# Filling matmuls of 512 and 256 columns in place of 128 in an attention and mixture-of-experts kernel

## The chip, the core and the metric

The kernel runs on one core of a Trainium2 chip. The metric is the device time of one execution in microseconds (us); several executions are timed and their median is given. One further execution is recorded by the hardware profiler, with its own time and its span, the stretch from the first to the last instruction of the program.

TensorE multiplies matrices (PE in the profile, PEld for its weight loads), VectorE is DVE, ScalarE is ACT, GpSimd is POOL, and SyncE (SP) issues nearly all data transfers.

## The reference

For each of 8 batches and 8 heads, a softmax over 32 memory slots pools keys and values, and the queries attend to the pooled ones:

```python
a = softmax(phi)                                  # (8, 8, 576, 32)
k_m = einsum('bhsm,bhsd->bhmd', a, k)             # pooled keys, 32 x 64
v_m = einsum('bhsm,bhsd->bhmd', a, v)
attn = softmax(q @ k_m.T / sqrt(64))
x = (attn @ v_m), laid out as (4608, 512)
```

The 4608 rows then go through a soft mixture of 8 experts with 4 slots each:

```python
logits = x @ phi_moe                              # (4608, 32)
slot_input = softmax_over_rows(logits).T @ x      # (32, 512)
slot_out[e] = relu(slot_input[e] @ w1[e]) @ w2[e] # 512 -> 1024 -> 512
out = softmax_over_slots(logits) @ slot_out       # (4608, 512)
```

All of it is float32.

## The kernel before

The work is put down as a list of operations, each with its engine, an assumed cost in us, the tiles it reads and writes, and a due time. A planner (`Plan.order`, L70, with `BatchPlan.order`, L256) simulates the engines and fixes the order in which each engine's instructions are issued; the order is static when the kernel runs. Each engine works through its own list in that order and waits where an input is late.

Per batch there are: the loads of phi, k, v and q (`load`, L481, all issued by SyncE; the DMA line in the profile is L483); the maximum of phi on VectorE (L536), its spreading by transposes and products on TensorE (L544, L558), the subtraction on GpSimd (L574), the exponential on ScalarE (L580), row sums on GpSimd (L587) and TensorE (L597); the pooling of keys and values as 144 small matmul records (L624); scaling on ScalarE (L640, L647), transposes (L658) and the routing product (L667); the scores (L735, two groups of 32 records), the softmax over VectorE, GpSimd and ScalarE (L749 to L799), transposes (L810), logits (L830), and the contribution to the slots (L913 to L963). Work of neighbouring batches overlaps. After the last batch the slot inputs are merged (SIM, L1096), the experts run (first layer L1163, second layer L1210) on weights that arrive 1 MB at a time in the arena space that the batches have left, and the output products (L1346) are copied and stored. L1317 is a product with 128x128 weights ahead of the output.

Where TensorE has no real work, the planner puts in filling products (`fill`, L497): products of a constant tile of ones by itself, into a PSUM bank that nothing reads. They have the priority `FILL`, behind all else, and every one is ready from the start. Two rules in `Plan.order` decide about them:

```python
look = self.LOOK if pri < FILL else self.FILL_LOOK      # 0.05 or 0.5
_, t, i = min(x for x in near if ops[x[2]][0] == e and x[1] <= t + look)
```

When a fill would be next, any real TensorE operation that is due within `FILL_LOOK` = 0.5 us is taken in its place; else one fill is issued and TensorE counts as taken for the fill's cost, `WC` = 0.3 us. Fills left over after the last real TensorE operation are dropped. `NWARM` = 250 are offered.

Of the kernel before, what the change touches and what calls it, by code (L numbers as in the profile page):

```python
# [16 lines left out]
PE, DVE, ACT, POOL, SP = range(5)  # L17
FILL = 10 ** 6


class Plan:
# [19 lines left out]
    def add(self, eng, cost, fn, r=(), w=(), also=(), pri=None, dma=0.0, slack=0.0):  # L41
        i = len(self.ops)
        deps = set()
        tiles = set()
        for x in r:
            for key in x:
                tiles.add(key[0])
                if key in self.last_w:
                    deps.add(self.last_w[key])
        for x in w:  # L50
            for key in x:
                tiles.add(key[0])
                if key in self.last_w:
                    deps.add(self.last_w[key])
                deps.update(self.reads.get(key, ()))
        for x in w:
            for key in x:
                self.last_w[key] = i
                self.reads[key] = []
        for x in r:  # L60
            for key in x:
                self.reads.setdefault(key, []).append(i)
        deps.discard(i)
        tiles = [t for t in tiles if t.pool is not None]
        for t in tiles:
            t.users += 1
        need = tiles + [t for t in also if t not in tiles]
        self.ops.append((eng, cost, fn, deps, i + self.bias if pri is None else pri, dma, tiles, need, slack))
# [212 lines left out]
def kernel(  # L281
# [30 lines left out]
    P = 128  # L312
# [28 lines left out]
    banks = [psum.tile([P, 512], F32, name=f"bank{i}") for i in range(4)]  # L341
# [56 lines left out]
    def entry(si):  # L398
# [36 lines left out]
    ident, maskhp, maskc, rep, repa, ones, mphd = (  # L435
        x.ap for x in (ident_b, maskhp_b, maskc_b, rep_b, repa_b, ones_b, mphd_b)
    )
    NWARM = 250
    WC = 0.3
    C_EXP = 0.8  # L440
    S_SLACK = 0.6

# [49 lines left out]

    warm = Tile(ap=banks[3][:, :P])

    def fill(n, pri, r=()):  # L497
        for _ in range(n):
            add(
                PE, WC,  # L500
                lambda: nc.tensor.matmul(  # L501
                    warm.ap, ones, ones,
                    start=True, stop=True,
                ),
                r=[ones_b, *r], w=[warm], pri=pri,
            )

    fill(NWARM, FILL)

    load(lambda: mphi_b.ap, moe_phi.rearrange("(c x) n -> x c n", x=P), 65536, mphi_b, pri=first("mphi"))  # L510

# [904 lines left out]
```

## Time and profile before

| What | us |
|---|---|
| median of 3 runs | 219.62 |
| lowest and highest | 218.26 to 220.39 |
| profiled execution, its own time | 218.71 |
| its span | 216.9 |
| TensorE busy (matmul) | 181.1 |
| VectorE busy | 135.9 |
| GpSimd busy | 88.9 |
| ScalarE busy | 83.0 |

The page shows busy times, then the span in 40 slices with a digit for the busy tenths of each; PEclk is the granted clock of TensorE in tenths. A row of a group or of the timeline has the engine, the source line, the operation, output and inputs by name, their shapes (for a matmul first the weights), and the count; the timeline puts start and length in us ahead, and in brackets behind how long the engine had stood idle and what ended that. "issue" stands where nothing that the profile records was waited for. A row of the windows has the stretch, its length, then for each engine the busy time with the number of instructions in brackets, then the granted clock, the DMA's share and its GB/s. A float32 product leaves two matmul records and two weight loads.

### The profile page before, as it was taken

How to read it: one execution, taken by the hardware profiler on the slowest of the kernel's cores; microseconds unless marked ns; L12 is line 12 of the kernel's file. 1: busy time of each engine (PE TensorE's matmuls, PEld its weight loads, DVE VectorE, ACT ScalarE, POOL GpSimd, SP SyncE). 2: the span in 40 equal slices, each digit the busy share in tenths (PEclk: the TensorE clock that was granted, in tenths of full speed). 3: DMA queues.
4: the chain of work that ended last, by engine and by line, in shares of the span. 5: the costliest groups of instructions: out<-in, count | busy, mean ns of one | idle time of the engine just before them, and what ended most of it. 6: DMA issues, size and time to landing. Idle time of an engine off the chain costs nothing.

```text
span 216.9 us, 6965 instructions
## 1 busy us (share of the span) xinstructions
PE 181.1 (83%) x3044; PEld 121.0 (56%) x3044; DVE 135.9 (63%) x246; ACT 83.0 (38%) x224; POOL 88.9 (41%) x96
## 2 busy tenths in 40 slices
PE   7697879979699989997999999989999967876700
PEld 6586559555366565654765657666555644643300
DVE  3335495988579798895759786549704850266700
ACT  2023306165066283672382946510102411146500
POOL 3381839487568575869265499000000000000000
PEclk9799997999979999997699999999999999999975
DMA  6999999999999999999943988699999999059997
GB/s 215 382 381 388 380 389 378 392 379 384 380 380 363 390 389 387 352 393 410 390 196 104 415 288 364 199 412 410 408 409 409 410 407 397 38 201 410 412 418 301
DMA packets 28174, 76.53 MB, mean 353 GB/s; under 512 B 1776, under 2 KB 5872, under 8 KB 28144
## 3 DMA queue, kind: packets, MB, share of 16 engines
q1 hardware_dynamic: 28144, 76.09, 92.6%
q8 instruction: 24, 0.39, 0.8%
q14 instruction: 6, 0.05, 0.1%
HBM read 66.65 MB, written 9.44 MB: 351 GB/s over the span
## 4 chain that ended last, share of the span: by engine, by line
PE 41%; DMA 19%; DVE 10%; ACT 8%; POOL 7%; SPq 6%; issue 4%; DVEq 0%; ACTq 0%; POOLq 0%
DMA arena<-in_moe_w_dram 11%; DMA arena<-in_phi_dram 8%; PE bank L1163 7%; PE kvbank L624 6%; PE scbank L735 6%; SPq L483 6%; PE bank L501 4%; DVE arena L1360 3%; PE scbank L1346 2%; PE bank L913 2%; PE kvbank L1210 2%; ACT arena L580 2%; PE bank L830 2%; POOL arena L794 2%; ACT arena L1358 2%
## 5 line engine op out<-in xcount | busy, mean ns | idle before, releaser
L501 PE MATMUL bank<-ones 128*128 128x128 f32 x232 | 38.6, 317 | 1.1 <-DVE ones L446 1.1
L501 PEld LDWEIGHTS bank<-ones 128*128 128x128 f32 x232 | 34.5, 227 | 4.2 <-issue 3.0
L587 POOL TENSOR_TENSOR arena<-arena 128x128 f32<-128x128 f32 (+2 forms) x32 | 23.4, 731 | 12.3 <-ACT arena L580 10.4
L703 DVE STREAM_TRANSPOSE arena<-top 128x1152 f32<-128x1152 f32 x16 | 21.7, 1360 | 10.6 <-DMA top<-in_q_dram 10.6
L574 POOL TENSOR_TENSOR arena<-arena 128x1152 f32<-128x1152 f32 x8 | 21.1, 2632 | 15.0 <-ACT arena L569 14.9
L771 POOL TENSOR_TENSOR arena<-arena,smx 128x576 f32<-128x576 f32 x16 | 18.5, 1159 | 14.3 <-DVE smx L766 14.3
L624 PE MATMUL kvbank<-arena 64*32 64x128 f32 x1152 | 21.9, 279 | 2.3 <-issue 1.2
L735 PE MATMUL scbank<-arena 32*32 32x288 f32 x512 | 21.2, 424 | 2.3 <-issue 2.1
L624 PEld LDWEIGHTS kvbank<-arena 64*32 64x32 f32 x1152 | 16.6, 107 | 7.4 <-issue 3.8
L749 DVE STREAM_TRANSPOSE arena<-scbank 128x576 f32<-128x576 f32 x16 | 12.3, 769 | 11.5 <-PE scbank L735 11.5
L815 ACT COPY arena<-bank 96x384 f32<-96x384 f32 x32 | 14.7, 483 | 12.3 <-PE bank L810 12.3
L536 DVE TENSOR_REDUCE arena<-arena 128x128 f32<-128x1152 f32 x8 | 17.4, 2179 | 2.6 <-DMA arena<-in_phi_dram 2.6
L794 POOL TENSOR_TENSOR arena<-arena,ssm 128x576 f32<-128x576 f32 x16 | 18.2, 1155 | 1.5 <-DVE ssm L790 1.3
L1210 PE MATMUL kvbank<-arena 128*32 128x256 f32 x256 | 16.1, 383 | 3.3 <-DMA arena<-in_moe_w_dram 3.2
L810 PE MATMUL bank<-ident,arena 128*96 128x128 f32 x96 | 16.0, 290 | 0.7 <-DVE arena L887 0.4
L799 DVE STREAM_TRANSPOSE arena<-arena 128x576 f32<-128x576 f32 x16 | 12.1, 758 | 5.1 <-POOL arena L794 5.1
L1163 PE MATMUL bank<-arena,SIM 128*32 128x256 f32 x256 | 14.2, 380 | 0.7 <-DVE SIM L1096 0.7
L735 PEld LDWEIGHTS scbank<-arena 32*32 32x32 f32 x512 | 8.1, 107 | 8.6 <-issue 3.1
L810 PEld LDWEIGHTS bank<-ident,arena 128*96 128x96 f32 x96 | 10.0, 132 | 5.0 <-issue 1.1
L1210 PEld LDWEIGHTS kvbank<-arena 128*32 128x32 f32 x256 | 7.3, 109 | 9.6 <-DMA arena<-in_moe_w_dram 5.3
L766 DVE TENSOR_REDUCE smx<-arena 128x18 f32<-128x576 f32 x16 | 11.8, 736 | 0.2
L776 ACT ACTIVATE arena<-arena 128x576 f32<-128x576 f32 x16 | 11.0, 690 | 2.1 <-POOL arena L771 2.1
(117 smaller groups left out, 266.1 us busy)
## 6 DMA issues: line engine op xcount, KB each, us to landing
arena<-in_moe_w_dram SPq DMA_DIRECT2D x32, 1024.0 KB, 11.2
arena<-in_k_dram SPq DMA_DIRECT2D x8, 1152.0 KB, 10.1
arena<-in_v_dram SPq DMA_DIRECT2D x8, 1152.0 KB, 12.6
top<-in_q_dram SPq DMA_DIRECT2D x8, 1152.0 KB, 11.0
out_dram<-arena SPq DMA_DIRECT2D x11, 768.0 KB, 6.5
arena<-in_phi_dram SPq DMA_DIRECT2D x8, 576.0 KB, 11.8
out_dram<-arena SPq DMA_DIRECT2D x3, 256.0 KB, 2.3
arena<-in_moe_phi_dram SPq DMA_DIRECT2D x1, 64.0 KB, 9.0
```

The costliest lines, as they stand in the source:

```text
L501: lambda: nc.tensor.matmul(warm.ap, ones, ones, start=True, stop=True,),
L536: lambda: nc.vector.tensor_reduce(mx.ap, ph().rearrange("p c j m -> p c m j"), axis=AX.X, op=ALU.max),
L574: lambda: nc.gpsimd.tensor_tensor(ph(), ph(), mb.ap.unsqueeze(2).to_broadcast([P, C, J, M]), op=ALU.subtract),
L587: plus = lambda o, x, y: nc.gpsimd.tensor_tensor(o, x, y, op=ALU.add)
L624: nc.tensor.matmul(acc.ap[M * c: M * c + M, a, : 2 * D], ph()[h0: h0 + HALF, c, j, :], kv()[h0: h0 + HALF, :, c, j * D: j * D + D], start= ...
L703: nc.vector.transpose(qT.ap.rearrange("p (i u y) -> p u i y", i=2, y=Y), qt.ap[:, h * QT_SZ: h * QT_SZ + QT_SZ].rearrange("p (u i x) -> p ...
L735: nc.tensor.matmul(scb.ap[M * c: M * c + M, r, :JY], kT.ap[h0: h0 + Y, i * P + M * c: i * P + M * c + M], qT[c // 2].ap.rearrange("p (i c ...
L771: lambda: nc.gpsimd.tensor_tensor(exv(), exv(), bc(mx), op=ALU.subtract),
L794: lambda: nc.gpsimd.tensor_tensor(exv(), exv(), bc(sm), op=ALU.mult),
L810: nc.tensor.transpose(tp.ap[:T, t * P: t * P + P], aT.ap[:, x: x + T], ident)
L1163: nc.tensor.matmul(hb.ap[NS * j: NS * j + NS, :256], SIM.ap[:, 2 * i + c, NS * e: NS * e + NS], wv[:, c, 256 * j: 256 * j + 256], start=(e ...
L1210: nc.tensor.matmul(pacc.ap[NS * x: NS * x + NS, h, :HD], hT()[:, 4 * t + i0 + j, NS * e: NS * e + NS], wv()[:, j, t, col: col + HD], start ...
```

## The change

`fill` takes a width. The first 14 fills multiply the ones by four copies of the ones side by side (512 columns, read by a broadcast), and the other 130 by two copies (256 columns). The assumed cost becomes 0.04 + 0.0021 times the columns: 1.115 us and 0.578 us. The tile that the fills write is the whole PSUM bank where it was its first 128 columns. Nothing else in the list of operations is changed; since the fills' costs enter the planner's simulation, the order of other work may come out otherwise.

```diff
-    NWARM = 250
-    WC = 0.3
+
+    NWIDE, NWARM = 14, 130
...
-    warm = Tile(ap=banks[3][:, :P])
-
-    def fill(n, pri, r=()):
+    warm = Tile(ap=banks[3])
+
+    def fill(n, w, pri, r=()):
         for _ in range(n):
             add(
-                PE, WC,
+                PE, 0.04 + 0.0021 * w,
                 lambda: nc.tensor.matmul(
-                    warm.ap, ones, ones,
+                    warm.ap[:, :w].rearrange("p (x y) -> p x y", y=P), ones,
+                    ones.unsqueeze(1).to_broadcast([P, w // P, P]),
                     start=True, stop=True,
                 ),
                 r=[ones_b, *r], w=[warm], pri=pri,
             )
 
-    fill(NWARM, FILL)
+    fill(NWIDE, 512, FILL)
+    fill(NWARM, 256, FILL)
```

## The prediction

> **What bounds the kernel now.** I read the page first, then the chain of work that ended last, then TensorE's timeline and the windows with their instruction counts.
>
> ```profile
> PE 181.1 (83%) x3044; PEld 121.0 (56%) x3044; DVE 135.9 (63%) x246; ACT 83.0 (38%) x224; POOL 88.9 (41%) x96
> PEclk9799997999979999997699999999999999999975
> q8 instruction: 24, 0.39, 0.8%
> PE 41%; DMA 19%; DVE 10%; ACT 8%; POOL 7%; SPq 6%; issue 4%; DVEq 0%; ACTq 0%; POOLq 0%
> L501 PE MATMUL bank<-ones 128*128 128x128 f32 x232 | 38.6, 317 | 1.1 <-DVE ones L446 1.1
> ```
>
> TensorE is the busiest engine and holds 41% of the chain. Its filling products (L501) are 232 of 3044 matmul records: a float32 product leaves two, each with a weight load, so 116 products ran, of the 250 allowed. The q8 row matters below: 24 packets carry 0.39 MB, about 16 KB each, while TensorE has 3044 + 3044 = 6088 instructions. That is 254 instructions, or 127 matmul records with their loads, to a packet.
>
> The chain shows the stages:
>
> ```profile
> 11.43 16.62 DMA arena<-in_phi_dram
> 28.07 2.12 DVE arena L536
> 56.33 1.72 issue
> 167.44 18.93 DMA arena<-in_moe_w_dram
> ```
>
> Until 28.07 us the inputs of the third batch set the pace: what TensorE does before that is covered by the DMA. Up to about 145 us the chain runs through the batches' work, much of it on TensorE. Late there means late release of the arena, hence late loading of the expert weights (last piece 167.44 + 18.93), and those loads end just before the outputs. So I carry lateness of TensorE between 31 and 107 us to the end one for one.
>
> The third row is the odd one: "issue", 1.72 us in which nothing seen was waited for. TensorE's timeline has seven such holes (brackets hold the idle time before the row):
>
> ```profile
> 26.38 1.73 PE L624 MATMUL kvbank<-arena 64*32 64x128 f32 x102 [0.76 <-issue]
> 45.48 0.16 PE L597 MATMUL bank<-maskhp,arena 128*128 128x2 f32 x1 [0.96 <-issue]
> 51.85 0.43 PE L624 MATMUL kvbank<-arena 64*32 64x128 f32 x10 [0.32 <-issue]
> 58.05 0.40 PE L735 MATMUL scbank<-arena 32*32 32x288 f32 x1 [1.72 <-issue]
> 72.53 1.19 PE L735 MATMUL scbank<-arena 32*32 32x288 f32 x29 [0.41 <-issue]
> 86.04 0.67 PE L624 MATMUL kvbank<-arena 64*32 64x128 f32 x30 [0.17 <-issue]
> 99.14 0.19 PE L935 MATMUL bank<-repa,arena 96*128 96x32 f32 x1 [1.16 <-issue]
> ```
>
> They cut runs of equal matmuls in two, so no data can be the reason. Counting TensorE's matmuls from the start up to the first, third, fourth and last hole (the count is in brackets), and taking one microsecond inside the fourth:
>
> ```profile
> 0.00:25.65 25.65, 20.91 (x349) 0.93 0.97 348
> 0.00:39.50 39.50, 32.45 (x603) 0.91 1.00 360
> 0.00:51.54 51.54, 43.07 (x857) 0.93 1.02 366
> 0.00:56.34 56.34, 47.55 (x985) 0.94 1.02 368
> 0.00:97.99 97.99, 85.70 (x1745) 0.95 1.03 373
> 57.00:58.00 1.00, 0.00 (x0) 0.00 (x0) 0.00 (x0) 0.00 (x0) 0.00 (x0) 1.00 1.06 359
> ```
>
> 349, 857, 985 and 1745 lie at multiples of 127 from one another (4 x 127 = 508; 128; 11 x 127 = 1397 against 1396). The holes are the edges of instruction packets: TensorE has used one up and the next has not come. From one edge to the next release passes 58.05 - 51.85 = 6.20 us and 51.85 - 45.48 = 6.37 us; the unheld edge at 603 was passed at 39.5 and the next opened at 45.48, 5.98 us later. So the rule I use is: an edge opens about 6.0 us after the last was passed, 6.2 if that one held, while the DMA is full (share 1.06 in the last row). A packet worked off faster ends in a hole. In the last row all five engines stand still: such a hole is not hidden.
>
> [...]
>
> **The change part by part.** First the number of fills. The planner takes a fill only when no real TensorE work is due within 0.5 us, and costs it at 0.3 us before, 0.04 + 0.0021 x 512 = 1.115 and 0.578 us after. Its gaps keep their length, so fewer, longer fills go in. The fills by stage:
>
> ```profile
> 0.00:7.00 7.00, 3.90 (x18) 3.71 (x18) 1.00 0.72 255
> 7.00:24.00 17.00, 9.34 (x58) 8.44 (x58) 0.90 1.07 385
> 24.00:39.20 15.20, 6.71 (x38) 6.24 (x38) 0.89 1.06 381
> 39.20:105.50 66.30, 5.57 (x32) 5.08 (x33) 0.93 1.04 383
> 105.50:146.00 40.50, 8.33 (x54) 6.85 (x53) 0.98 0.77 289
> ```
>
> To 7 us: 9 fills, 2.7 us of plan, become 3 wide ones. To 24 us: 29 fills, 8.7 us, lie in seven gaps, five of them of one or two fills which still take one whole wide fill, so 11 and not 8. That uses up all fourteen. To 39.2 us: 19 fills, 5.7 us, become 10 of 256 columns; to 105.5 us 16 become about 10. In records, 76 - 28 = 48 are gone by 24 us, 114 - 48 = 66 by 39 us, about 78 by 105.5 us.
>
> Second, the time that fills hold TensorE. Warm, the row of 128 columns at 189.06 (below) has 8 records in 1.05 us, about 0.13 each, 0.25 us a product, 0.83 of its planned 0.3. The nearest row for 256 columns with 128x128 weights is L1317 at 188.12: 4 records before the next start at 189.06, 0.235 each, 0.47 us a product, 0.81 of the planned 0.578. A straight line gives 0.9 us for 512 columns, 0.81 of the plan. Time per planned gap is thus the same: nought, bounds -1 us (two per cent of 38.6 busy, rounded up) and +1 us (a fill of 512 overshoots its gap by up to 0.6 us, and the gaps before 28 us lie under the DMA; only the short gaps after it count, with 0.08 us each).
>
> Third, the edges. With 48 to 68 records gone, each edge falls on later work. The first then lies near 349 + 50, inside the x102 run of L624; a hole like the longest seen is covered by VectorE's piece that starts at 28.07 and takes 2.12, on which TensorE waits anyway. For the next ones I take counts from before at the places where they land:
>
> ```profile
> 0.00:37.80 37.80, 30.75 (x543) 0.91 1.00 359
> 0.00:40.40 40.40, 33.35 (x666) 0.92 1.00 361
> 0.00:50.40 50.40, 41.94 (x799) 0.93 1.02 366
> 0.00:54.50 54.50, 45.72 (x922) 0.94 1.02 367
> ```
>
> The edge at 476 lands on 476 + 66 = 542, passed at 37.8; the next opens at 43.8. The edge at 603 lands on 669, reached at 40.4 after a dense run of L624 and L735: a hole of 3.4 us. The edge at 730 lands on 798. Before needs 10.0 us from 40.4 to there, 0.96 of it a hole, so 9.04: reached at 52.8, open since 43.8 + 6.2 = 50.0, no hole. The edge at 857 lands on 925; 4.1 - 0.32 = 3.8 us later, at 56.6, while it opens at 52.8 + 6.0 = 58.8: a hole of 2.2 us. Together 5.6 us against 0.96 + 0.32 + 1.72 = 3.0 before: +2.6 us. The later holes I take as they are (0.41 + 0.17 + 1.16), since a batch is a little over two packets and the edges drift through it in either kernel. Bounds: -4.7 (all holes after 39 us gone) and +4.
>
> Fourth, the clock. It fell to half after two of the holes, and these pairs show the same work at half and at full clock:
>
> ```profile
> 60.84 1.50 PE L830 MATMUL bank<-arena 128*32 128x192 f32 x12
> 74.02 0.85 PE L830 MATMUL bank<-arena 128*32 128x192 f32 x12
> 100.10 2.17 PE L735 MATMUL scbank<-arena 32*32 32x288 f32 x32
> 96.33 1.20 PE L735 MATMUL scbank<-arena 32*32 32x288 f32 x32
> 102.20 1.53 PE L624 MATMUL kvbank<-arena 64*32 64x128 f32 x48
> 94.20 0.94 PE L624 MATMUL kvbank<-arena 64*32 64x128 f32 x48
> 104.76 1.92 PE L501 MATMUL bank<-ones 128*128 128x128 f32 x8
> 189.06 1.05 PE L501 MATMUL bank<-ones 128*128 128x128 f32 x8
> 188.12 1.10 PE L1317 MATMUL bank<-arena,rep 128*128 128x256 f32 x4 [0.64 <-DVE arena L1312]
> ```
>
> The losses are 0.65 + 0.97 + 0.59 + 0.87 = 3.1 us, over one dip near 60 us and one twice as long from 100 us: about 1.0 us for each of three stretches. With two large holes instead I expect two stretches, 2.1 us: -1.0 us. Bounds: -3.1 (no dip left) and +2 (two stretches more).
>
> The sum: 0 + 2.6 - 1.0 = +1.6 us. The profiled execution took 218.71 us with a span of 216.9; with the term it is 220.3. It was below the median of the runs, 219.62; against that the forecast is **221.2 us**, 0.7% slower.
>
> **The rivals.** *The edges land well and the clock holds.* Fewer instructions pass through the same slow door, and an edge that falls beside fills or a wait costs nothing, as 603 did before. If all holes after 39 us (4.7) and all dips (3.1) went, 7.8 us were won; half of that is 3.9, **215.7 us**. For it speaks that the planner may order real work otherwise once its gaps are filled differently, which moves edges; against it that the first landing place, a dense run of L624 between 37.8 and 40.4, needs a shift of some thirty records to be left. *A long hole throws the clock.* A hole of 3.4 us is twice the 1.72 that was followed by a dip; if from 44 us each large hole brings a dip of two stretches, as from 100 us, there are four to five stretches in place of three: 2.6 + 2.0 = +4.6, **224.2 us**. It decides from the point where a hole outlasts about 1.2 us, the shortest that a dip followed. *The holes are hidden anyway,* because VectorE, at 63%, has queued work when TensorE stands; then only fills change, and **219.6 us** stays. The all-still row at 57 us speaks against it.
>
> **How the numbers follow.** A measurement of this kernel tells about 1% from no change, that is below 217.4 or above 221.8. The forecast case has 0.38 with its own range of 219 to 223.5 (same 0.17, slower 0.18, faster 0.03 by its bounds). The edges that land well: 0.36 (faster 0.34, same 0.02). The thrown clock: 0.15, slower. Hidden holes: 0.11 (same 0.08, slower 0.02, faster 0.01). Sums: faster 0.38, same 0.27, slower 0.35. The range reaches into the first rival down to 214.5 and over the second up to 224.5.
>
> **What would show it.** Right: some 58 fills, 14 of them wide and all before 24 us; TensorE 100 to 130 matmul records fewer and 23 packets; holes at counts 127 apart that stand on later work, the largest, 2 to 4 us, near 41 to 44 us and a second near 57; one-stretch dips behind them. Wrong: no hole above 1 us, or holes of that size with the other engines busy throughout; or the real work of TensorE in another order, so that the counts lead to other places; or a time below 217.4.

## The result and the profile after

The changed kernel takes 229.87 us in the median of four executions (226.21 to 232.91), the kernel before 220.0 (218.26 to 221.78). The ratio is 1.038 with a 95% interval of 1.028 to 1.049; a second measurement of the same two (experiment 12) gave 1.028, 1.019 to 1.038. Ratios compare the undisturbed executions of both kernels, which is why one can lie below the ratio of the medians. The profiled execution took 226.21 us with a span of 224.4; before it was 218.71 with 216.9.

The page of the changed kernel, in the lines that answer to those of before:

```profile
span 224.4 us, 6728 instructions
PE 186.9 (83%) x2926; PEld 110.8 (49%) x2926; DVE 137.5 (61%) x246; ACT 82.7 (37%) x224; POOL 88.7 (40%) x96
PEclk9999999889999659979999999999999988999985
q8 instruction: 23, 0.38, 0.7%
PE 50%; DMA 16%; DVE 10%; ACT 9%; issue 6%; SPq 5%; POOL 1%; ACTq 0%; DVEq 0%
L501 PE MATMUL bank<-ones 128*128 128x256 f32 (+1 forms) x114 | 45.3, 516 | 1.1 <-DVE ones L446 1.1
```

118 matmul records are gone (3044 to 2926) and one instruction packet (24 to 23). TensorE's share of the chain rose from 41% to 50%, and "issue", the idle time that nothing explains, from 4% to 6%.

Next the holes in TensorE's timeline, and the number of its matmuls up to the start of each:

```profile
28.49 1.06 PE L626 MATMUL kvbank<-arena 64*32 64x128 f32 x52 [1.43 <-issue]
42.65 0.84 PE L626 MATMUL kvbank<-arena 64*32 64x128 f32 x35 [3.10 <-issue]
58.77 0.67 PE L737 MATMUL scbank<-arena 32*32 32x288 f32 x4 [1.21 <-issue]
72.02 0.85 PE L626 MATMUL kvbank<-arena 64*32 64x128 f32 x38 [1.91 <-issue]
88.86 0.44 PE L626 MATMUL kvbank<-arena 64*32 64x128 f32 x13 [1.51 <-issue]
```

```profile
0.00:27.06 27.06, 23.02 (x349) 1.00 0.98 349
0.00:39.54 39.54, 33.15 (x604) 1.00 1.01 361
0.00:57.56 57.56, 47.30 (x858) 0.97 1.02 368
0.00:70.11 70.11, 58.21 (x1112) 0.98 1.03 372
0.00:87.36 87.36, 73.55 (x1366) 0.92 1.01 365
```

349, 604, 858, 1112, 1366: the same ladder of 127 records as before (349, 603, 857), now on other work. In sum the holes are 1.43 + 3.10 + 1.21 + 1.91 + 1.51 = 9.2 us, against 5.5 before.

The trace also shows what ends a hole. In the changed kernel, packets of queue q8 end at 27.15, 41.42, 57.31, 70.56 and 87.47 us, and TensorE goes on at 28.49, 42.65, 58.77, 72.02 and 88.86, that is 1.2 to 1.5 us after each. The fourteen traces of this case have 80 holes of more than 0.15 us with "issue" as releaser; every one of them ends 1.2 to 1.6 us after a packet of q8 has ended, and all stand within a few records of the same ladder of 127. So the holes are waits for the next packet of instructions.

The clock is lower too; the windows show where it was granted at half:

```profile
43.50:46.90 3.40, 3.40 (x16) 0.50 1.08 381
46.90:74.20 27.30, 22.98 (x536) 1.00 1.04 383
74.20:84.40 10.20, 10.20 (x63) 0.50 1.01 356
84.40:94.70 10.30, 8.74 (x253) 1.00 0.60 204
91.30:94.70 3.40, 3.35 (x67) 1.00 1.01 386
94.70:98.10 3.40, 3.40 (x20) 0.50 1.06 401
```

The counts of these windows cannot be compared, since the work in them differs. The same twelve records at full and at half clock can:

```profile
61.51 0.85 PE L832 MATMUL bank<-arena 128*32 128x192 f32 x12
75.74 1.50 PE L832 MATMUL bank<-arena 128*32 128x192 f32 x12
```

The stretches at half clock are 3.40, 10.20 and 3.40 us long in these windows; the second is counted as three. What brings a fall the windows do not settle: the one at 43.5 came behind a hole of 3.10 us, the one at 74.2 behind one of 1.91, and in the 3.4 us ahead of the fall at 94.7 TensorE was busy for 3.35. The holes of 1.43 and 1.21 us had no stretch at half clock behind them before the next hole. So that a hole brings the fall is a guess that fits the stretches at 43.5 and 74.2, and not all.

### The profile page after: what moved, and what is told of

It is laid out like the page before. It is cut to its first block, busy times and chain, and to the rows that moved or that the text cites. A ratio compares the mean times of both kernels' runs of the same rounds, so it can differ in the third digit from the quotient of the medians.

```text
span 224.4 us, 6728 instructions
## 1 busy us (share of the span) xinstructions
PE 186.9 (83%) x2926; PEld 110.8 (49%) x2926; DVE 137.5 (61%) x246; ACT 82.7 (37%) x224; POOL 88.7 (40%) x96
## 4 chain that ended last, share of the span: by engine, by line
PE 50%; DMA 16%; DVE 10%; ACT 9%; issue 6%; SPq 5%; POOL 1%; ACTq 0%; DVEq 0%
DMA arena<-in_moe_w_dram 8%; PE scbank L737 8%; DMA arena<-in_phi_dram 7%; PE bank L501 6%; PE kvbank L626 6%; PE bank L1165 6%; SPq L483 5%; PE bank L812 4%; PE bank L915 3%; PE bank L832 3%; PE kvbank L1212 3%; DVE arena L1362 3%; PE scbank L1348 2%; PE bank L937 2%; ACT arena L1360 2%
## 5 line engine op out<-in xcount | busy, mean ns | idle before, releaser
L501 PE MATMUL bank<-ones 128*128 128x256 f32 (+1 forms) x114 | 45.3, 516 | 1.1 <-DVE ones L446 1.1
L501 PEld LDWEIGHTS bank<-ones 128*128 128x128 f32 x114 | 21.9, 219 | 10.6 <-issue 8.0
L773 POOL TENSOR_TENSOR arena<-arena,smx 128x576 f32<-128x576 f32 x16 | 18.5, 1158 | 10.6 <-DVE smx L768 10.5
L737 PE MATMUL scbank<-arena 32*32 32x288 f32 x512 | 20.5, 407 | 1.5 <-issue 1.2
L1212 PE MATMUL kvbank<-arena 128*32 128x256 f32 x256 | 16.9, 398 | 3.3 <-DMA arena<-in_moe_w_dram 3.3
L812 PE MATMUL bank<-ident,arena 128*96 128x128 f32 x96 | 16.8, 299 | 1.0 <-ACT arena L817 0.2
L812 PEld LDWEIGHTS bank<-ident,arena 128*96 128x96 f32 x96 | 10.9, 139 | 5.7 <-ACT arena L817 2.5
L1212 PEld LDWEIGHTS kvbank<-arena 128*32 128x32 f32 x256 | 7.5, 112 | 10.2 <-DMA arena<-in_moe_w_dram 5.0
L783 DVE TENSOR_REDUCE ssm<-arena 128x18 f32<-128x576 f32 x16 | 11.6, 737 | 0.8 <-ACT arena L778 0.7
```

What stands on the lines that cost most here:

```text
L501: lambda: nc.tensor.matmul(warm.ap[:, :w].rearrange("p (x y) -> p x y", y=P), ones, ones.unsqueeze(1).to_broadcast([P, w // P, P]), start= ...
L737: nc.tensor.matmul(scb.ap[M * c: M * c + M, r, :JY], kT.ap[h0: h0 + Y, i * P + M * c: i * P + M * c + M], qT[c // 2].ap.rearrange("p (i c ...
L773: lambda: nc.gpsimd.tensor_tensor(exv(), exv(), bc(mx), op=ALU.subtract),
L812: nc.tensor.transpose(tp.ap[:T, t * P: t * P + P], aT.ap[:, x: x + T], ident)
L1212: nc.tensor.matmul(pacc.ap[NS * x: NS * x + NS, h, :HD], hT()[:, 4 * t + i0 + j, NS * e: NS * e + NS], wv()[:, j, t, col: col + HD], start ...
```

## The experiments

Three theories stood against each other. *Edges:* taking records out of TensorE's stream moves the ends of its instruction packets onto dense work; the holes there, and the clock after them, cost the time. *Plan:* the new costs made the planner order the real work otherwise, and that costs it. *Width:* wide fills stand in front of real work. The planner's order of the real work is the same up to 30 us and differs from there; for one thing, before splits the 72 products of L624 in the third batch into 24 and 48 around a group of scores, after issues them in one run. TensorE has 2812 records of real work in every kernel. Where two kernels share the plan, these records come in the same order, and record by record the traces tell how late one is against the other.

**1 to 4: the same plan with other edges, and the other way round.** The first three keep the plan of after, with all planned costs, and issue its fills in narrower pieces; the fourth keeps the plan of before and issues its fills merged.

```diff
-    fill(NWIDE, 512, FILL)
+    fill(8, 512, FILL, pieces=4)      # 1; in 2 and 3 all 14
+    fill(6, 512, FILL)
     fill(NWARM, 256, FILL)            # 3: pieces=2
```

> The plan, the order of all operations and the fills' planned costs are those of after; only the first eight wide fills are issued as four products of 128 columns each, which puts 48 matmul records back into TensorE's stream before the third batch, as many as the change took out by 24 us. Theory of the edges (the change costs what it costs because instruction packets end at other places, each such end opens a hole, and the holes drop the clock): by the rule of 5.7 to 6.2 us from edge to edge the holes after 32 us shrink from 7.7 us to about 4 to 5 us, the dips of the clock from five stretches of 3.4 us to two or three, and the time falls to 220 to 224 us. Rival of the plan (the other order of real work costs the time): it stays with after, 226 to 231 us. Rival of the width (wide fills stand ahead of real work): about half of the difference is won back, 224 to 226 us.

> As the first kernel of this set, but all fourteen wide fills are issued as four products of 128 columns: 84 records more than after. Theory of the edges: 84 records carry the edges past the good place again; holes after 32 us about 1.5 to 2 us fewer than after's 7.7, time 224 to 228 us, so slower than the kernel with eight split. Rival of the plan: as after, 226 to 231 us. Rival of the width: the fastest of the two splits, since no wide product is left, 220 to 223 us.

> The plan of after, but every fill is issued in pieces of 128 columns (four for a wide one, two for one of 256), so no wide product is left at all and TensorE has more instructions than before. Theory of the edges: the largest holes of all (about 1 us more than after, over 3 us each near 30 and 44 us), time 227 to 232 us. Rival of the width: the loss is gone, 219 to 222 us. Rival of the plan: as after, 226 to 231 us.

```diff
+    GAPS = (9, 1, 15, 1, 7, 1, 2, 2, 2, 2, 11, 4)   # runs of fills; 4 become one of 512, 2 one of 256
+    # the first of a merged group issues the wide product, the others nothing
```

> The plan and the order of all real work of before, with the same planned costs of its fills; only the first 57 fills are issued merged within their runs (four as one product of 512 columns, two as one of 256), which takes out 68 records by 39 us, as many as the change does. Theory of the edges: the holes of before move to those that the prediction worked out, 2 to 3.4 us near 41 to 45 us and 2 us near 57 us; 2 to 4 us more of holes and one or two dips more, 222.5 to 227 us. Rival of the plan: as before, 218 to 221 us. Rival of the width: slower by less than 1 us, 220 to 221 us, as the wide ones lie before 39 us.

Measured: 227.04 us (221.43 to 227.3) with eight split; 235.46 us, ratio 1.068 (1.056 to 1.080) with fourteen; 236.45 us, ratio 1.065 (1.054 to 1.077) with all fills narrow; and 225.68 us, ratio 1.024 (1.014 to 1.034) for before with merged fills. The kernel before ran at 220.44 beside them.

Of the four expectations of the edges only the last was met. The kernel with eight split missed it: its holes sum to 7.7 us where 4 to 5 were expected, seven stretches at half clock stand where two or three were, and its time lies inside what the rival of the plan had named. The other two are slower than expected, with holes of 11.4 and 15.9 us and eleven stretches each.

Taken together the four still decide. The width as the sole cause falls: the kernel without a wide product is the slowest. The plan as the sole cause falls too, since one plan gives 227, 235 and 236 us, and the plan of before loses 2.4% with nothing changed but how its first fills are cut. The records of real work show where the time goes. With fourteen split, the hundredth is 0.1 us later than in the changed kernel; behind the hole of 2.64 us below the two-hundredth is 3.1 us later, and behind that of 3.55 us, with half clock after it, the four-hundredth 8.3. In the merged kernel the five-hundredth is 0.4 us earlier than in before; behind the hole of 2.94 us, with half clock after it, the six-hundredth is 3.6 later. The holes of the merged kernel, and the counts ahead of the first three:

```profile
28.19 1.11 PE L633 MATMUL kvbank<-arena 64*32 64x128 f32 x58 [2.08 <-issue]
43.31 0.41 PE L633 MATMUL kvbank<-arena 64*32 64x128 f32 x3 [2.94 <-issue]
59.98 0.66 PE L633 MATMUL kvbank<-arena 64*32 64x128 f32 x29 [1.69 <-issue]
```

```profile
0.00:26.10 26.10, 22.72 (x349) 1.00 0.98 349
0.00:40.35 40.35, 33.49 (x604) 1.00 1.01 362
0.00:58.28 58.28, 48.29 (x857) 0.94 1.02 365
```

The second and third are the prediction's two holes, near where it had them and each half a microsecond shorter (3.4 at 40.4, 2.2 at 56.6). My size for the second kernel was wrong, 224 to 228 against 235: five holes of up to 3.5 us, two of which fall before 35 us, and long stretches at low clock:

```profile
19.40 0.27 PE L600 MATMUL bank<-maskhp,arena 128*128 128x2 f32 x1 [2.64 <-issue]
34.35 0.63 PE L627 MATMUL kvbank<-arena 64*32 64x128 f32 x2 [3.55 <-issue]
64.80 0.45 PE L627 MATMUL kvbank<-arena 64*32 64x128 f32 x16 [1.05 <-issue]
76.85 1.41 PE L738 MATMUL scbank<-arena 32*32 32x288 f32 x26 [1.27 <-issue]
108.28 1.88 PE L916 MATMUL bank<-arena 96*32 96x258 f32 x12 [2.86 <-issue]
```

Its granted clock, from the page:

```profile
PEclk9997985799999659998559999999999999999985
```

**5: the kernel before with more records.**

```diff
+    widths = [(64, 64)] * 22          # the first 22 fills as two products of 64 columns
```

> The plan and order of before; its first 22 fills are issued as two products of 64 columns in place of one of 128, which adds 44 records to TensorE's stream by 13 us. No product is wider than before. Theory of the edges: this too carries the edges off their good places, to the other side; by the rule of 5.7 to 6.2 us from edge to edge the holes after 25 us grow by 4 to 5 us, with one to three stretches of low clock more, 224 to 230 us. Rivals of the plan and of the width: nothing that they name is changed, 218 to 222 us.

Measured: 234.12 us, ratio 1.056 (1.046 to 1.066), beyond the expected range. It is not a clean case: the split fills hold TensorE longer. The hundredth record of real work starts at 24.72 us where it started at 14.68 before. At the three-hundredth, at 34.48 us and still ahead of the first hole, 7.7 of the 18 us that it is late at the end are there. So this run does not show what edges moved the other way cost. Experiments 10 and 11 repeat it with the fills left whole.

**6: late fills left out.**

```diff
+    widths = [(P,)] * 57 + [()] * 16  # the sixteen fills between 39 and 106 us issue nothing
```

> The plan and order of before; the sixteen fills that stand between 39 and 106 us are left out of TensorE's stream, with their planned time kept, so that it has 32 records fewer there and all edges before 39 us stay. Theory of the edges: the same work passes through fewer packets; holes after 39 us fall from 4.7 us to about 2, 215 to 219 us. Rival of the clock (late fills are what holds the clock up): more stretches at half clock than the four of before, 221 to 226 us.

Measured: 223.95 us, ratio 1.015 (1.004 to 1.026). The expectation of the edges was wrong here, and the time is the one that the rival of the clock had named. The trace shows both at work: the stream was 32 records shorter, but one hole grew from 0.32 to 2.50 us (7.9 us of holes in all against 5.5), and after it half clock lasted for 13.7 us (the digits 5, 5 and 7). Up to 190 us there are six stretches at half clock, against five before:

```profile
53.92 0.41 PE L623 MATMUL kvbank<-arena 64*32 64x128 f32 x4 [2.50 <-issue]
```

Its granted clock, from the page:

```profile
PEclk9699988999557999999999999999999999999675
```

That no fill was there to bring the clock back is not shown: a stretch just as long stands in experiment 12, which has its fills. Nor is the large hole one of an edge on denser work: TensorE comes to it at 51.42 us as before (51.53), but the packet that ends it starts 6.0 us after the release ahead of it (45.31), where it started 3.9 us after it before. Why it came late stays open. Fewer instructions alone did not help here.

**7 and 8: a lighter DMA.** In both kernels the loads of k and v are left out from the third batch on.

```diff
+            if b < 2:
                 load(lambda i=i: kv()[:, i], rows(src, b), ...)
+            else:
+                add(SP, 0.06, lambda: None, w=[kb.part(i)], ...)
```

> The changed kernel, with the loads of k and v left out from the third batch on (the products then read the data of the first two batches), 14 MB less for the DMA; TensorE's instructions and their order are the same. Theory of the edges: the next packet is late because it queues behind the data; with a lighter DMA the holes that stood at 28, 42, 58, 72 and 88 us (9.2 us together) shrink to under 3 us, and the difference to the next kernel, before with the same loads out, falls from 8 us to 0 to 3 us. Rival of a fixed price (an edge costs its 6 us whatever the DMA does): holes of 1.2 to 3.1 us stay at the same counts. Rival of the plan: holes go, and the difference of 8 us stays.

> The kernel before, with the same loads of k and v left out from the third batch on. Theory of the edges: its holes (5.5 us together) go as well, and it gains less by it than the changed kernel does. Rival of a fixed price: its seven holes stay. Rival of the plan: it stays 6 to 10 us faster than the changed kernel with the same loads out.

Measured: 229.3 us for the changed kernel, as with all loads; 216.49 us, ratio 0.986 (0.978 to 0.994), for the one before. The holes of the changed kernel did not shrink, 10.2 us in sum, so my expectation failed. Nor did the kernel before gain less than the changed one: it gained 1.4%, with six holes of 4.0 us in sum, and lies 12.8 us below it in the medians, more than the rival of the plan had named. A reason why the holes stayed is offered by the trace: the loads that remain run just when TensorE is dense. In this kernel, the stretch ahead of the hole that ended at 42.21, the hole itself, and the time behind it:

```profile
42.21 0.84 PE L629 MATMUL kvbank<-arena 64*32 64x128 f32 x35 [2.67 <-issue]
87.57 0.44 PE L629 MATMUL kvbank<-arena 64*32 64x128 f32 x11 [3.33 <-issue]
```

```profile
37.00:39.00 2.00, 2.00 (x122) 1.00 1.03 391
40.00:42.00 2.00, 0.00 (x0) 1.00 0.00 0
42.21:43.30 1.09, 1.09 (x36) 1.00 0.00 0
43.30:44.50 1.20, 1.20 (x10) 1.00 0.08 14
```

Ahead of the hole, from 37 to 39 us, the DMA was full (1.03). From 43.3 us on the DMA carries 14 GB/s for 1.2 us, one packet of 16 KB and nothing else: with an idle DMA (0.00 from 42.21 to 43.3) the next packet moves 1.1 us after the release at 42.21. In the kernel before, with the DMA full, the q8 queue carried nothing from the release at 45.48 up to 49.3, and in the window from 45.48 to 49.4 this, its next packet:

```profile
q8 instruction: 1, 0.02, 1.7%
```

That is some 3.8 us after the release. So, as an estimate from these two packets, 2.7 of the 6.2 us go with the full DMA. The other 3.5 us are there with an idle DMA too: the 1.1 us until the packet moves, and, in the changed kernel with all loads, 1.1 us while a packet moves (86.38 to 87.47 us, with the DMA at 0.12) and 1.4 us from its end to the release at 88.86 (with the DMA at 0.00). The rival of a fixed price is half right; in the changed kernel what it had named came true, holes of 1.23 to 3.33 us at nearly the same counts.

**9 to 11: more records, with the fills left whole.** Products of one element by one element stand behind some of the early fills. They were meant to give TensorE next to no work and only to take their place in the stream.

```diff
+                for _ in range(thin):  # 9: 7 behind 4 wide fills of after; 10: 2 behind 11, 11: 1 behind 10 fills of before
+                    nc.tensor.matmul(warm.ap[:1, :1], ones[:, :1], ones[:, :1], start=True, stop=True)
```

> The changed kernel, plan, order and all fills as they are; behind each of four wide fills stand seven products of one element by one element, which put 56 records into the stream before 13 us and give TensorE next to nothing to do. Theory of the edges, as it now stands (span = 207.5 us + the holes + 1.0 us for each stretch of 3.4 us at half clock + 2.4 us where the changed order of real work is used): holes after 25 us of about 6 us in place of 9.2, three to five stretches, span 218 to 222, time 220 to 224 us, against 226 to 231 us for the changed kernel. Rival of the plan alone or of the width alone: 226 to 231 us, since neither is touched.

> The kernel before; two products of one element by one element stand behind each of eleven fills, 44 records before 13 us. The fills stay as wide as they are, so that the clock comes up early as in before. Theory of the edges: holes of about 10 us in place of 5.5, six to eight stretches of low clock, time 224 to 229 us. Rivals of the plan and of the width: 218 to 222 us.

> As the kernel with 44 records more, but with 20. Theory of the edges: between the two, holes of about 7 to 8 us, four to six stretches, 220 to 224 us. Rivals of the plan and of the width: 218 to 222 us.

Measured: the changed kernel with 56 empty records more takes 224.85 us in the median of ten (221.04 to 226.51), ratio 1.012 (1.006 to 1.019), a little above the expected range. About half of the loss is won back by products whose results nobody reads; the changed kernel had 226.21 to 233.66 in its eight executions. Its holes after 25 us sum to 6.4 us, as expected, but one of 3.03 us stands ahead of them, and seven stretches at half clock in place of three to five. Where the five microseconds were won the trace does not tell, since the profiled execution took 225.88 us, close to the 226.21 of the changed kernel's.

The kernel before with 44 takes 227.98 us, ratio 1.029 (1.023 to 1.035), as expected, with holes of 9.3 us. With 20 it takes 231.89 us (229.32 to 234.84), not between the two as I expected, but above, with holes of 8.6 us. Neither is a test of the edges alone. This is the stretch of the early fills with 44 (before, the granted clock was 0.90 in it):

```profile
7.00:24.00 17.00, 16.79 (x233) 13.28 (x234) 5.20 (x6) 1.43 (x2) 6.33 (x8) 0.60 1.06 384
```

With 20 it was 0.60 as well. From 8.6 us a fill with its two empty products follows the last by 0.89 us, with its one by 0.85, where a fill took 0.33 before. The hundredth record of real work is 7.3 us late with 44 and 7.0 with 20, ahead of any hole; at the three-hundredth 4.8 and 5.5 us are left (with 20, a hole of 1.13 us lies between). At the end of the real work they are 9.0 and 10.6 us late. So up to about half of these two losses may be the early low clock and the long fills, which I had not reckoned with. The holes and the clock with 20:

```profile
37.55 0.60 PE L500 MATMUL bank<-ones 128*128 128x128 f32 x3 [2.72 <-issue]
62.50 2.13 PE L734 MATMUL scbank<-arena 32*32 32x288 f32 x21 [1.77 <-issue]
79.39 0.85 PE L623 MATMUL kvbank<-arena 64*32 64x128 f32 x17 [1.70 <-issue]
```

Its granted clock, from the page:

```profile
PEclk9656998899959959999679999999999999999975
```

**12: the changed kernel again.**

> The changed kernel once more, unchanged. Theory of the edges: the holes lie at the same counts of instructions and take the same time, within 1 us in sum, in every execution; what differs from execution to execution is how many stretches of low clock follow them, and the time follows these by about 1 us each. Rival: other holes, or the same stretches with another time.

Measured: 229.87 us (226.62 to 233.66), span of the profiled execution 227.0. The holes stand at the same work:

```profile
28.21 1.06 PE L626 MATMUL kvbank<-arena 64*32 64x128 f32 x52 [1.22 <-issue]
42.63 1.49 PE L626 MATMUL kvbank<-arena 64*32 64x128 f32 x35 [3.07 <-issue]
58.74 0.67 PE L737 MATMUL scbank<-arena 32*32 32x288 f32 x4 [1.25 <-issue]
73.06 1.37 PE L626 MATMUL kvbank<-arena 64*32 64x128 f32 x38 [1.53 <-issue]
91.12 0.44 PE L626 MATMUL kvbank<-arena 64*32 64x128 f32 x13 [1.16 <-issue]
110.26 0.71 PE L737 MATMUL scbank<-arena 32*32 32x288 f32 x7 [0.32 <-issue]
```

Its granted clock, from the page:

```profile
PEclk9999999799799558999799999999999988999985
```

They sum to 8.6 us against 9.2, and the execution is still 2.6 us longer: its stretches at half clock are eight up to 190 us, against six. Holes and stretches together explain 1.4 of the 2.6 us, so the expectation holds to about a microsecond.

**The account.** Taking from each span its holes and 1 us for each stretch at half clock between 7 and 190 us:

| Kernel | span | holes | stretches | rest |
|---|---|---|---|---|
| before | 216.9 | 5.5 | 5 | 206.4 |
| before, 57 fills merged | 222.9 | 7.5 | 7 | 208.4 |
| before, late fills out | 221.4 | 7.9 | 6 | 207.5 |
| before, 44 more | 225.9 | 9.3 | 8 | 208.6 |
| before, 20 more | 227.5 | 8.6 | 11 | 207.9 |
| before, 22 fills split | 235.0 | 8.3 | 11 | 215.7 |
| before, k and v out | 214.4 | 4.0 | 2 | 208.4 |
| after | 224.4 | 9.2 | 6 | 209.2 |
| after again | 227.0 | 8.6 | 8 | 210.4 |
| after, 8 split | 225.5 | 7.7 | 7 | 210.8 |
| after, 14 split | 232.1 | 11.4 | 11 | 209.7 |
| after, all narrow | 236.6 | 15.9 | 11 | 209.7 |
| after, 56 more | 224.1 | 9.4 | 7 | 207.7 |
| after, k and v out | 225.0 | 10.2 | 6 | 208.8 |

But for one kernel, spans from 214 to 237 us leave rests between 206 and 211. The one is before with 22 fills split, which holds TensorE longer ahead of all holes (experiment 5). Without it the plan of before leaves 207.9 in the mean, that of after 209.5; with it, 209.0. Of the 7.5 us between the two profiled spans, 3.7 are holes, 1 is the clock, and some 2.8 are left. The 1 us was chosen to fit, and rests of one plan differ by 2 to 3 us among themselves. That what is left is the new order is a guess from this table, and no run isolates it. At the five-hundredth record of real work the changed kernel is even 1.3 us ahead (38.37 against 39.67 us), at the two-thousandth 5.9 us behind, so whatever the order costs it costs after 38 us. Why the clock falls after one hole for one stretch and after another for three stays open too.

## Why the prediction was wrong

*Right.* The mechanism: edges of instruction packets that stand on other work, with the largest hole of about the size forecast, and lateness carried to the end (the last piece of the weights ends at 185.9 us before and at 193.0 after). The direction was hardly forecast: 0.7% slower lay inside what the prediction calls no change, and its chances had 0.38 for faster and 0.35 for slower. The fills: 57 products ran (114 records) where 58 were worked out, thirteen of the fourteen wide ones by 24.4 us and the last at 29.48. By 39 us 76 records were gone where 66 were worked out. The time a wide fill takes: two rows of after,

```profile
20.98 1.02 PE L501 MATMUL bank<-ones 128*128 128x512 f32 x2
48.90 0.62 PE L501 MATMUL bank<-ones 128*128 128x256 f32 x2
```

whose followers start at 21.93 and 49.41, so 0.95 and 0.51 us a product, near the 0.9 and 0.47 expected. The first edge was hidden at its hole of 1.43 us, as said: in the chain of the changed kernel VectorE's piece stands at 28.07 with 2.18 us, and TensorE comes in only at 34.49. The great hole of 3.4 us near 41 to 44 us came as one of 3.10, ended at 42.65; the second, 2.2 us near 57, came as 1.21, at 57.56. It ended where it was worked out, 58.77 against 58.8, but TensorE reached it a microsecond later than forecast. The sum of these two was 4.3 where 5.6 was worked out.

*Wrong, a sentence of the third step:* "The later holes I take as they are". Before they were 0.41 + 0.17 + 1.16 = 1.74 us, after 1.91 + 1.51 = 3.42. The ladder of 127 goes on and every rung falls on other work; it has to be followed to the end of the stage. All holes after 39 us rose by 3.0 us (4.7 to 7.7), against +2.6 forecast, so this step's total was near by luck: the first two holes came 1.3 us short and the later ones 1.7 us long.

*Wrong, the fourth step,* in its sign: "I expect two stretches, 2.1 us: -1.0 us". I let each large hole bring one stretch of low clock. After had five between 39 and 107 us where before had three, about +2 us in place of -1.0, three of them in a row behind a hole of 1.91 us; the second profiled execution had seven up to 115 us. The rival of the thrown clock (224.2 us) was the nearer case; it had 0.15.

*Wrong by omission:* the order of real work. The prediction names it as something that would lead the counts elsewhere, and gives it no price. What holes and clock leave over, some 2.8 us of the 7.5 between the profiled spans, may be its price; that stays open.

*The range.* Its upper end, 224.5 us, joined +2.6 of holes with +2.0 of clock. The holes could be +4 by the prediction's own bounds, and the order had no bound at all. Even the profiled execution, 226.21 and the shortest of its four, lies above that end.

## What to carry to other kernels

Where TensorE runs long series of small matmuls beside a busy DMA, count its instructions. Here the 80 holes of more than 0.15 us with no releaser stood on a ladder of 127 matmul records, each ended 1.2 to 1.6 us after an instruction packet had, and a change of the stream ahead, be it of dummy work, put those behind it on other work. Check a gain or loss from such a change by shifting the stream before believing in its reason, and then see that what was put in or taken out does not itself hold TensorE or its clock: compare the start of the same real work ahead of the first hole (with 22 fills split, the hundredth record came at 24.72 us in place of 14.68). The low clock could not be priced here from the length of a hole: 1.91 us had three stretches behind it, 1.21 none, and one came behind 3.4 us in which TensorE was busy for 3.35. Give it a bound on the upper side.

## What the runs showed that I had not expected

Twenty records of empty products (0.7% of TensorE's stream) cost the kernel before some 5% (220.22 to 231.89 us), part of it perhaps by the low clock ahead of the first holes, and 56 of them won the changed kernel from 229.87 to 224.85 us. From the release of a hole to the next packet's start 1.1 us passed with an idle DMA (0.00, after k and v out, from 42.21 us) and some 3.8 us with a full one (1.07, before, from 45.48 us). In all fourteen traces TensorE ran dry at ends of instruction packets, on the ladder of 127 matmul records.
